# Rounding angles inside PSUM and packing small matmuls: an adaLN block with a state-space convolution

## The chip, the cores and the metric

The kernel runs on one core of a Trainium2 chip. The metric is the device time of one execution in microseconds. The engines named below are PE (TensorE: matmuls into PSUM), DVE (VectorE), ACT (ScalarE), POOL (GpSimd) and SP (SyncE, which here only issues DMAs, in order). Each engine works through its own instructions in order, and waits for others by semaphores. PSUM has eight banks of 128 x 512 fp32; this kernel uses six as a rotating pool ("pb", by the function `bank`) and two for the angles ("pa").

## The reference

The input x is 2048 rows (positions) of 512 channels. Six vectors of 512 come from `mod = silu(c) @ w_mod`: shift, scale and gate for two halves. The first half normalizes each row, scales and shifts it, and convolves each channel along the positions with its own kernel K; the second is an MLP.

```python
h = _layernorm(x) * (1 + ca) + sa
x = x + ga * _A_ref(h, ...)        # convolution with K, plus h * Dskip
h = _layernorm(x) * (1 + cb) + sb
x = x + gb * _B_ref(h, ...)        # Dense 512->1792, Mish, Dense 1792->512

# inside _A_ref, for each channel d and position l (N = 128 states):
P = jnp.exp(logdA[:, :, None] * l[None, None, :])     # complex
K = jnp.einsum("dn,dnl,dn->dl", Cc, P, dB).real
y = irfft(rfft(pad(u)) * rfft(pad(K)))[:L]            # linear convolution by FFT of 4096
```

P needs a magnitude (an exponential) and a phase (sine and cosine of an angle counted in turns, so only its fractional part matters).

## The kernel before, in words

**Blocks and steps.** The 512 channels are four blocks b of 128. Each block has eight groups of 16 channels, so there are 32 groups, and the main loop walks steps k = -1 to 40. A step runs one stage of each of many pipelines, each at its own offset (the table `ORDER`): for example the angles of group k+2, the kernel generation of group k-1, the Fourier stage of piece k-7. Every instruction gets a priority, 10000 times the step plus a fraction (`PRI0` for steps below 7, `PRI` later, otherwise the place in `ORDER`). A planner then lays out each engine's order and the turns of the buffers from these priorities with a cost model of its own.

**Angles (s_ang, s_ri, s_neg, s_sin).** For each group, PE forms 2 x 512 angles per partition as x, in turns, by four fp32r matmuls of 256 columns with the table `ac` (L341) into the two "pa" banks, of which there is one set. Then the whole number of turns is taken off. Adding and subtracting MAGIC = 1.5 * 2^23 in fp32 rounds to an integer. For 14 of the 32 groups (`RID` = 1) DVE does both at once, out of PSUM (L352). For the other 18, ACT adds MAGIC (L346) and DVE subtracts it (L354). The rounded value goes back to PE, which subtracts it by two fp16 matmuls with minus the identity (L359, `negid`). ACT then reads the angles as an absolute value (L364) and as a sine, which frees the banks, and makes the cosine from the first.

**Kernel generation.** DVE makes the magnitudes (s_mag, L374 and L377) and multiplies them in (s_comb, L384 to L388); PE contracts over the states (s_kgen, L399; 32-column outputs in four column groups) and does the first part of the Fourier transform of K (s_ka, L416). ACT copies in between.

**Input.** `stats` takes means and variances of 16 tiles XR[j] of 128 positions (12 on DVE, group 3 on ACT), `norm_scales` the reciprocal roots, `norm` (L505) normalizes in place. `ua(j, hf)` multiplies a tile by a 128 x 128 constant `bdu` on PE (L512), ACT copies the bank (L513), and after each second tile SP writes to the DRAM scratch `ud` (L515). These stand in steps 1 to 4. From step 6 on, `s_gl` reads `ud` back in another order.

**Modulation.** For each vector four pieces of w_mod come in; for each, four f32 matmuls use the piece as weights and move a single column (L445), ACT copies 4 columns (L449), and `mod_sum` on DVE adds the pieces.

**Fourier stage and back.** For each piece v (32 in all) PE transforms input and kernel (s_ubu, s_ubk, L530), DVE multiplies (s_prod), PE transposes (s_t1), inverts (s_invb, L579), ACT copies, SP writes to scratch `zd` (L582; two halves for each block). For each block, after its eight pieces, s_zl reads it back as `zt` in four tiles (L590; the halves land in a tile's two rows of 512), s_inva does the last inverse by two f32 matmuls of 128 rows and 512 columns for each tile (L614), DVE adds the input (L616, loaded by s_xp through `x_rows`, L192) and SP writes x2d (L617).

**Tail and MLP.** After the loop the last block's zl and inva, the second layernorm (ln_stats, ln_norm, ln_t) and the MLP over four tiles of 512 positions (L868, L886).

An f32 matmul shows in the trace as two records, each with its own weight load; fp32r, bf16 and fp16 ones as one.

Of the kernel before, what the change touches and what calls it, by code (L numbers as in the profile page):

```python
# [10 lines left out]
F32 = mybir.dt.float32  # L11
# [7 lines left out]
P = 128  # L19
# [15 lines left out]
BN = [0, 0, 0, 1]  # L35
NS = 1
SPA = 0
RID = [1, 0, 0, 0, 1, 0, 0, 0, 1, 0, 0, 0, 1, 0, 0, 1, 1, 0, 0, 0, 1, 1, 0, 1, 1, 0, 1, 0, 1, 1, 0, 1]
PRI = {"mm": 0.933, "ug": 0.775, "tm": 0.608, "inva": 0.817, "sin": 1.075, "ml": 0.533, "st": 0.933, "par": 0.625, "ri": -0.108, "kgen": 0.05, "p": -0.475, "sr": 1.575, "t2": 0.15, "ls": 0.275, "ut": 0.675}
PRI0 = {"comb": 0.675, "mc": 0.133, "sm": -0.167, "ua": 0.008, "par": 0.675, "ut": 0.583, "mm": 0.383, "inva": 1.717, "ka": 1.258, "ang": 0.067, "neg": 0.533, "ri": -0.067, "mag": 0.467}  # L40
# [6 lines left out]
    ("kgen", 1), ("ks", 1), ("ubu", 7), ("ang", -2), ("gl", 6), ("ri", -2), ("misc", 0), ("zl", 13),  # L47
    ("mag", -1), ("t1", 9), ("ka", 1), ("par", 0), ("tm", 1), ("neg", -2),
# [4 lines left out]
def _constants():  # L53
# [14 lines left out]
    di = np.zeros((2, 2, 4, 16, 32, 4))  # L68
    for t in range(4):
        bdk[t, :, :, t, :] = da  # L70
        for hf in range(2):
            for c in range(2):
                di[hf, c, t, :, :, t] = da[:, c, 16 * hf:16 * hf + 16].T / 2048.0
    bdu = bdk.transpose(1, 0, 2, 3, 4)
# [13 lines left out]
    for e in range(3):  # L88
# [13 lines left out]
        "bdu": np.ascontiguousarray(bdu.reshape(P, 8, 2, 16).transpose(0, 2, 3, 1)).reshape(P, 256).astype(f),  # L102
        "di": np.ascontiguousarray(di.transpose(3, 1, 2, 0, 4, 5)).reshape(P, 256).astype(f),
# [14 lines left out]
def s4_block(ctx, tc, io, out):  # L118
# [71 lines left out]
    def x_rows(dst, j0, n, b=None):  # L190
        w = D if b is None else P
        nc.sync.dma_start(dst, view(io["A_u"], j0 * D + (0 if b is None else b * P),  # L192
                                    [[16 * D, P], [D, n], [1, w]]))

    bdk = cst.tile([P, 256], F32, name="bdk")
    bdu = cst.tile([P, 256], F32, name="bdu")
    di = cst.tile([P, 256], F32, name="di")
# [9 lines left out]
    negid = gen.tile([P, P], F16, name="negid", bufs=1)  # L207
    magic = const_col(MAGIC, "magic")
# [123 lines left out]
    EC, PA, RI, MG = {}, {}, {}, {}  # L332

    def s_ang(k):
        b, c = divmod(k, 8)
        p = psum.tile([P, 2, 512], F32, tag="pa", name="pang", bufs=1)
        PA[k] = p
        for e in range(2):
            for q in range(2):
                g, o = 2 * q + c // 4, 8 * (c % 4)  # L340
                T.matmul(p[:, e, 256 * q:256 * q + 256], S12[b, g][:, e, :],  # L341
                         ac[:, 32 * o:32 * o + 256], start=(q == 0), stop=False, skip_group_check=True)
        EC[k] = gen.tile([P, 2, 16, 96], F32, tag="ec", name=f"ec{k}", bufs=3)
        if RID[k]:
            return
        A.activation(EC[k][:, :, :, 32:64], p.rearrange("p e (d x) -> p e d x", d=16), AF.Identity, bias=magic)  # L346

    def s_ri(k):
        ri = gen.tile([P, 2, 512], F16, tag="ri", name=f"ri{k}", bufs=1)
        RI[k] = ri  # L350
        if RID[k]:
            V.tensor_scalar(ri, PA[k], MAGIC, MAGIC, op0=OP.add, op1=OP.subtract)  # L352
            return
        V.tensor_scalar(ri.rearrange("p e (d x) -> p e d x", d=16), EC[k][:, :, :, 32:64], MAGIC, None,  # L354
                        op0=OP.subtract)

    def s_neg(k):
        for e in range(2):
            T.matmul(PA[k][:, e, :], negid, RI[k][:, e, :], start=False, stop=True, skip_group_check=True)  # L359

    def s_sin(k):
# [3 lines left out]
        act(ang[1], pv, AF.Sin, scale=TWO_PI)  # L365
# [67 lines left out]
    WM = {}  # L433
    mcol = gen.tile([P, 24, KB], F32, name="mcol", bufs=1)
# [7 lines left out]
    def mod_mm(n):  # L442
        p = bank("pmodp")
# [4 lines left out]
    def mod_cp(n):  # L448
        A.copy(mcol[:, n, :], WM[n][:, :NB])  # L449

    def mod_sum(s):
        t = mcol[:, 4 * s:4 * s + 4, :]
        V.tensor_add(t[:, 0:2], t[:, 0:2], t[:, 2:4])
        V.tensor_add(modp[:, s, :], t[:, 0], t[:, 1])
        if s in (2, 3):
            V.tensor_scalar(modp[:, s, :], modp[:, s, :], 1.0, None, op0=OP.add)
# [43 lines left out]
    SEG = 16 * P  # L500
    ud = dram.tile([2 * NB * P, SEG], F32, name="ud")
    zd = [[dram.tile([P, 16, P], F32, name=f"zd{b}{hf}") for hf in range(2)] for b in range(NB)]
# [4 lines left out]
    def ua(j, hf):  # L507
        if j % 2 == 0:
            US[j // 2, hf] = cv.tile([P, NB, 2, P], F32, tag="us", name=f"us{j}{hf}", bufs=2)
        t = US[j // 2, hf]  # L510
        p = bank("pua")
        T.matmul(p, bdu[:, P * hf:P * hf + P], XR[j], start=True, stop=True)  # L512
        A.copy(t[:, :, j % 2, :], p.rearrange("p (b d) -> p b d", b=NB))  # L513
        if j % 2:
            nc.sync.dma_start(view(ud, hf * NB * P * SEG + (j - 1) * P, [[SEG, P], [P * SEG, NB], [1, 2 * P]]),  # L515
                              t.rearrange("p b j d -> p b (j d)"))
# [456 lines left out]
```

## Time and profile before

| what | us |
|---|---|
| three runs | 749.09, 754.63, 756.65 (median 754.63) |
| the profiled execution | 749.49 |
| its span (first to last instruction) | 747.7 |
| busy in the span: PE, DVE, ACT | 659.3, 455.7, 358.4 |
| mean granted clock of PE | 0.966 |

A row of a group of instructions reads: line, engine, operation, out<-in, shapes, count | busy time in us, mean ns of one | idle time of that engine just before them, and what ended it. A row of the timeline reads: start, duration (both us), engine, line, and in brackets the idle time before and who ended it. A row of waits reads: who <- for whom, total us, how often, longest.

### The profile page before, as it was taken

Reading aid. Unit: us, or ns where it says so; the run is one execution under the profiler, and the core shown is the slowest. Engines: PE = TensorE matmul, PEld = TensorE weight load, DVE = VectorE, ACT = ScalarE, POOL = GpSimd, SP = SyncE. Lnnn points to the kernel's source line nnn. Section 1 sums busy time; section 2 is a strip of 40 time slices with the busy share of each in tenths; the row PEclk is TensorE's granted clock in tenths of the full one; section 3 lists DMA queues with packets and bytes.
Section 4 is the critical chain, followed back from the end, with each engine's and each line's share of the span. In section 5 each row is a group of like instructions: output and inputs, shape, how many; then the busy total and the mean of one; then the engine's idle time right before and its main releaser. Section 6 shows DMA issues by size and latency. Waiting matters only on the chain.

```text
span 747.7 us, 13563 instructions
## 1 busy us (share of the span) xinstructions
PE 659.3 (88%) x5472; PEld 517.5 (69%) x5472; DVE 455.7 (61%) x940; ACT 358.4 (48%) x565; POOL 51.7 (7%) x108
## 2 busy tenths in 40 slices
PE   0781998899987998999996699999999999999997
PEld 0560456688765777777764378888888888888885
DVE  5879726888999999999663785138111521152113
ACT  4753566887886688765552262232223322232221
POOL 1005002024203220000000000000000000000000
PEclk9985899899999999999999899999999999999999
DMA  9752575245424762355685760003100320002001
GB/s 307 248 196 46 159 263 156 72 121 141 123 58 115 195 173 73 104 167 170 200 265 169 232 205 1 0 2 121 47 1 0 106 64 1 0 12 74 0 1 57
DMA packets 87751, 83.09 MB, mean 111 GB/s; under 512 B 8836, under 2 KB 69256, under 8 KB 87048
## 3 DMA queue, kind: packets, MB, share of 16 engines
q1 hardware_dynamic: 80968, 78.35, 33.2%
q0 software_dynamic: 6720, 3.87, 2.9%
q8 instruction: 43, 0.70, 0.4%
q14 instruction: 20, 0.16, 0.1%
HBM read 54.93 MB, written 25.17 MB: 107 GB/s over the span
## 4 chain that ended last, share of the span: by engine, by line
PE 69%; DVE 16%; DMA 7%; ACT 6%; issue 1%; POOL 0%; SPq 0%; DVEq 0%; ACTq 0%; POOLq 0%
PE pm L868 20%; PE po L886 19%; PE pka L416 3%; PE pua L512 3%; PE pkg L399 3%; PE pub L530 3%; PE pkb L530 3%; PE pmodp L445 2%; PE pib L579 2%; PE pia L614 2%; DVE ec L388 2%; PE pang L341 2%; DVE q L564 2%; DVE ec L384 2%; PE pang L359 1%
## 5 line engine op out<-in xcount | busy, mean ns | idle before, releaser
L875 DVE TENSOR_TENSOR mal<-mh,mah 128x512 fp32r<-128x512 f32 x56 | 38.6, 691 | 177.1 <-ACT mah L874 176.7
L868 PE MATMUL pm<-hh,w1h 128*128 128x512 f32 x448 | 139.3, 392 | 2.8 <-ACT hh L779 2.8
L142 ACT ACTIVATE mh<-pm,b 128x512 f32<-128x512 f32 x56 | 38.5, 690 | 202.7 <-PE pm L868 202.7
L868 PEld LDWEIGHTS pm<-hh,w1h 128*128 128x128 f32 x448 | 84.6, 189 | 21.3 <-ACT hh L779 3.3
L868 PE MATMUL pm<-hh,w1l 128*128 128x512 f32 x224 | 87.9, 392 | 0.0
L886 PE MATMUL po<-w2h,mah 128*128 128x512 f32 x224 | 87.9, 392 | 0.0
L886 PE MATMUL po<-w2l,mah 128*128 128x512 f32 x224 | 87.6, 391 | 0.0
L886 PE MATMUL po<-w2h,mal 128*128 128x512 f32 x224 | 87.3, 390 | 0.0
L384 DVE TENSOR_TENSOR ec<-ec,m 128x1024 f32<-128x1024 f32 x32 | 39.0, 1219 | 20.0 <-ACT ec L142 19.8
L868 PEld LDWEIGHTS pm<-hh,w1l 128*128 128x128 f32 x224 | 42.5, 190 | 8.9
L886 PEld LDWEIGHTS po<-w2h,mah 128*128 128x128 f32 x224 | 42.0, 188 | 8.8 <-issue 0.4
L886 PEld LDWEIGHTS po<-w2h,mal 128*128 128x128 f32 x224 | 42.0, 188 | 8.5
L886 PEld LDWEIGHTS po<-w2l,mah 128*128 128x128 f32 x224 | 42.1, 188 | 8.3
L564 DVE TENSOR_TENSOR q<-pkb,ug 128x512 f32<-128x512 f32 x64 | 41.8, 683 | 6.3 <-PE pkb L530 6.2
L399 PE MATMUL pkg<-ec 128*32 128x64 f32 x2048 | 40.2, 228 | 4.5 <-DVE ec L388 4.5
L512 PE MATMUL pua<-xr,bdu 128*128 128x512 f32 x64 | 31.6, 642 | 13.6 <-DVE xr L505 13.1
L416 PE MATMUL pka<-bdk,ks 128*64 128x128 f32 x512 | 39.8, 286 | 3.4 <-DVE ks L405 3.4
L399 PEld LDWEIGHTS pkg<-ec 128*32 128x32 f32 x2048 | 34.4, 112 | 11.6 <-issue 7.3
L364 ACT ACTIVATE ec<-pang 128x1024 f32<-128x1024 f32 x32 | 32.9, 1027 | 15.0 <-PE pang L359 14.8
L530 PE MATMUL pkb<-mf,gk 128*128 128x128 f32 x256 | 37.8, 284 | 1.8 <-ACT gk L423 1.8
L374 DVE TENSOR_TENSOR m<-co 128x1024 f32<-128x1024 f32 x32 | 39.0, 1219 | 0.1
L388 DVE TENSOR_TENSOR ec<-ec,m 128x1024 f32<-128x1024 f32 x32 | 38.9, 1217 | 0.0
(164 smaller groups left out, 1154.6 us busy)
## 6 DMA issues: line engine op xcount, KB each, us to landing
ud<-us SPq DMA_DIRECT2D x16, 512.0 KB, 3.5
gu<-ud SPq DMA_DIRECT2D x32, 256.0 KB, 2.9
zd<-z SPq DMA_DIRECT2D x32, 256.0 KB, 2.6
zt<-zd SPq DMA_DIRECT2D x32, 256.0 KB, 4.1
wm<-in_w_mod SPq DMA_DIRECT2D x24, 256.0 KB, 2.9
out<-ot SPq DMA_DIRECT2D x16, 256.0 KB, 2.0
xp<-in_A_u SPq DMA_DIRECT2D x15, 256.0 KB, 3.3
x2d<-xp SPq DMA_DIRECT2D x15, 256.0 KB, 3.5
```

The costliest lines, as they stand in the source:

```text
L142: chain(A.activation(out, in_, f, **kw))
L374: V.tensor_mul(m2.rearrange("p d (a b) -> p d a b", a=8), co[:, :, 12:20, None].to_broadcast([P, 16, 8, 8]), co[:, :, None, 20:28].to_broa ...
L384: V.tensor_mul(ec[:, :, :, 32:64], ec[:, :, :, 95:63:-1], m2[:, None, :, 0:32].to_broadcast([P, 2, 16, 32]))
L388: V.tensor_mul(ec[:, :, :, 0:32], ec[:, :, :, 0:32], m1[:, None].to_broadcast([P, 2, 16, 32]))
L399: T.matmul(o, ec[:, z, e, 0:32], ec[:, z, e, 32:96], start=(z == 0), stop=(z == 1))
L416: T.matmul(pv[64 * cc:64 * cc + 64, :, o:o + 4], KS[k][:, 64 * m:64 * m + 64], bdk[:, 128 * cc:128 * cc + 128], start=True, stop=True)
L512: T.matmul(p, bdu[:, P * hf:P * hf + P], XR[j], start=True, stop=True)
L530: T.matmul(pv[:, :, r, :], lh(r), mf[:, 4 * s + r, :].rearrange("p (c s) -> p c s", c=2), start=not started, stop=True, skip_group_check=s ...
L564: V.tensor_mul(q, kv[:, c, :, None, :].to_broadcast([P, 4, 2, 64]), ug)
L868: T.matmul(p, w1[wi][:, k, fs], hh[:, hi, k, :], start=(n == 0), stop=(n == 3 * KB - 1))
L875: V.tensor_sub(a[1], h, a[0])
L886: T.matmul(PO[tt][q], a[ai][:, P * q:P * q + P], w2[wi][:, f, :], start=(f == 0 and n == 0), stop=(f == FB - 1 and n == 2))
```

## The change

1. **Angles.** s_ri and s_neg go, and with them the ACT pass of s_ang. Everything becomes one accumulation in PSUM: x by `ac` (four matmuls), plus MAGIC and minus MAGIC as two bf16 matmuls of 512 columns for each half (ones times MAGIC/128 over 128 rows), minus x by `nac` = -`ac` (four matmuls). What stays is round(x) - x, and the sine's scale turns its sign.
2. **Input.** Positions are laid out anew over the partitions (32 rows of 64 positions each, four groups a). `ua(g)` multiplies 32 rows by 64 columns: eight f32 matmuls in four row groups and two column halves, into four banks at once; four ACT copies into tiles borrowed from several tags; eight DMAs of 512 B runs to `ud`.
3. **Last inverse.** zd is one scratch per block; a `zt` tile holds two column halves of 64 rows; s_inva works on pairs of the former tiles: eight matmuls of 64 rows and 32 columns into two banks. x_rows of one block becomes four DMAs.
4. **Modulation.** The vector silu(c) is the weight (32 equal columns), the w_mod piece moves, 512 columns, the four pieces in four column groups of one bank; one ACT copy; the sum over the groups by four matmuls against a column of 1/32 and one DVE operation.
5. **Order.** stats(3) moves to step 0, norm_scales and norm get priorities ahead (-0.6, -0.4) in step 1, ua gets 0.7 in place of 0.008 and goes by g, two per step; the load order of the tiles changes.

```diff
-BN = [0, 0, 0, 1]
+BN = [0, 0, 0, 0]
-PRI0 = {"comb": 0.675, "mc": 0.133, "sm": -0.167, "ua": 0.008, ...
+PRI0 = {"no": -0.6, "nr": -0.4, "comb": 0.675, "mc": 0.133, "sm": -0.167, "ua": 0.7, ...
...
+        for a in range(4):
+            nc.sync.dma_start(dst[32 * a:32 * a + 32], view(io["A_u"], (16 * a + j0) * D + b * P,
+                                                            [[64 * D, 32], [D, n], [1, P]]))
...
+        o = 8 * (c % 4)
         for e in range(2):
-            for q in range(2):
-                g, o = 2 * q + c // 4, 8 * (c % 4)
-                T.matmul(p[:, e, 256 * q:256 * q + 256], S12[b, g][:, e, :],
-                         ac[:, 32 * o:32 * o + 256], start=(q == 0), stop=False, skip_group_check=True)
+            for w in (ac, nac):
+                for q in range(2):
+                    T.matmul(p[:, e, 256 * q:256 * q + 256], S12[b, 2 * q + c // 4][:, e, :],
+                             w[:, 32 * o:32 * o + 256], start=(w is ac and q == 0), stop=(w is nac),
+                             skip_group_check=True)
+                for z in range(2) if w is ac else ():
+                    T.matmul(p[:, e, :], oneb.to_broadcast([P, P]), rnd[:, z:z + 1].to_broadcast([P, 512]),
+                             start=False, stop=False, skip_group_check=True)
...
-        act(ang[1], pv, AF.Sin, scale=TWO_PI)
+        act(ang[1], pv, AF.Sin, scale=-TWO_PI)
...
     def mod_mm(n):
-        p = bank("pmodp")
-        for b in range(NB):
-            T.matmul(p[:, b:b + 1], WM[n][:, b * P:b * P + P], sc[:, n % KB:n % KB + 1], start=True, stop=True)
-        WM[n] = p
+        s, k = divmod(n, KB)
+        if k == 0:
+            PM[s] = bank("pmodr")
+        T.matmul(PM[s][32 * k:32 * k + 32, :], sc[:, k:k + 1].to_broadcast([P, 32]), WM[n], start=True, stop=True)
...
-    def ua(j, hf):
...
+    def ua(g):
+        ps = [bank("pua") for a in range(4)]
+        for h in range(2):
+            for a in range(4):
+                r = slice(32 * a, 32 * a + 32)
+                T.matmul(ps[a][64 * h:64 * h + 64, :], bdu[r, :], XR[8 * h + g][r, :], start=True, stop=True)
+        for a in range(4):
+            tag = ("us", "ug", "us", "xp", "ug", "us", "xp", "q1")[(4 * g + a) % 8]
+            t = cv.tile([P, NB, P], F32, tag=tag, name=f"us{g}{a}", bufs={"us": 3, "q1": 1}.get(tag, 2))
+            A.copy(t.rearrange("p b d -> p (b d)"), ps[a])
+            for h in range(2):
+                nc.sync.dma_start(view(ud, (16 * a + 8 * h + g) * P, [[64 * P, 64], [64 * 64 * P, NB], [1, P]]),
+                                  t[64 * h:64 * h + 64])
...
-        p = bank("pia")
-        for hf in range(2):
-            T.matmul(p, di[:, P * hf:P * hf + P], ZT[b, j4][:, hf, :], start=(hf == 0), stop=(hf == 1))
+        ps = [bank("pia") for h in range(2)]
+        for a in range(4):
+            for h in range(2):
+                r = slice(64 * h, 64 * h + 64)
+                T.matmul(ps[h][32 * a:32 * a + 32, :], di[r, :], ZT[b, j4 - 1, a // 2 * 2][r, a % 2, :], start=True, stop=True)
...
-    for n, j in enumerate((12, 13, 14, 15, 8, 9, 10, 11, 0, 1, 2, 3, 4, 5, 6, 7)):
-        at(NS, norm, j)
-        for hf in range(2):
-            at(NS + n // 4, ua, j, hf)
+    for n, g in enumerate((4, 5, 6, 7, 0, 1, 2, 3)):
+        for h in range(2):
+            at(NS, norm, 8 * h + g)
+        at(NS + UO + n // 2, ua, g)
```

More of the change, by code (lines that the diff above doesn't have):

```diff
@@ L206, in s4_block @@
     halfpi = const_col(HALF_PI, "halfpi")
-    negid = gen.tile([P, P], F16, name="negid", bufs=1)
-    magic = const_col(MAGIC, "magic")
+    oneb = cst.tile([P, 1], BF16, name="oneb")
+    nc.gpsimd.memset(oneb, 1.0)
+    rnd = cst.tile([P, 2], BF16, name="rnd")
+    for z in range(2):
+        nc.gpsimd.memset(rnd[:, z:z + 1], (1 - 2 * z) * MAGIC / P)
+    nac = gen.tile([P, 1024], F32R, name="nac", bufs=1)
     dt = cst.tile([P, NB], F32, name="dt")
@@ L635, in s4_block @@
     params(0, 3)
-    V.tensor_scalar(negid, ident, -1.0, None, op0=OP.mult)
+    V.tensor_scalar(nac, ac, -1.0, None, op0=OP.mult)
     load_s(0, 0)
```

119 lines of the change are left out of this document (46 added, 73 removed).

## The prediction

> **What bounds the kernel now.** I read the page first, its 40 slices, then a table of busy times by stage (columns: stretch, length, then busy time and instruction count of PE, PEld, DVE, ACT and, where it works, POOL; granted clock, DMA share, GB/s).
>
> ```profile
> span 747.7 us, 13563 instructions
> PE   0781998899987998999996699999999999999997
> ```
>
> ```profile
> core 0: us, PE busy (x) PEld busy (x) DVE busy (x) ACT busy (x) POOL busy (x), PEclk, DMA share, GB/s
> 0.00:39.00 39.00, 15.63 (x52) 11.37 (x52) 28.77 (x111) 21.45 (x41) 2.80 (x12) 1.00 0.79 267
> 39.00:121.00 82.00, 62.41 (x549) 37.94 (x548) 55.08 (x132) 42.65 (x77) 12.21 (x24) 0.83 0.53 172
> 121.00:180.00 59.00, 53.06 (x757) 43.67 (x757) 48.45 (x92) 47.08 (x78) 16.36 (x32) 0.94 0.44 119
> 180.00:340.00 160.00, 146.13 (x2122) 116.59 (x2123) 156.72 (x249) 121.23 (x177) 20.35 (x40) 0.99 0.45 125
> 340.00:426.00 86.00, 67.53 (x598) 49.99 (x596) 57.21 (x119) 34.44 (x53) 0.00 (x0) 0.96 0.66 203
> 426.00:747.70 321.70, 314.52 (x1400) 257.91 (x1400) 109.48 (x241) 91.56 (x141) 0.00 (x0) 0.99 0.13 44
> ```
>
> The last row is the MLP, PE at 98%; the change leaves its instructions alone (only the rows of the output move). So everything happens in the first 426 us, and there no one engine rules. In 39 to 121 us (where the input is transformed) no engine is over 76% busy. In 180 to 340 us DVE is 98% busy and idle for 3.3 us in all, with PE close behind at 91%. In 340 to 426 us neither is full.
>
> Slice 3 of the PE line is a 1. The waits of PE in that place, and the timeline, name the cause:
>
> ```profile
> PE pua L512 <- DVE xr L505: 13.1, 2, 12.7
> ```
>
> ```profile
> 73.84 1.22 PE L512 MATMUL pua<-xr,bdu 128*128 128x512 f32 x1 [12.70 <-DVE xr L505]
> ```
>
> The input matmuls stand in PE's order ahead of everything else of their step, and wait 12.7 us for normalized rows that DVE reaches late.
>
> **The change part by part.** First what can be priced from rows; the lines by form give count, busy time and mean ns.
>
> ```profile
> L512 PE MATMUL pua<-xr,bdu 128*128 128x512 f32 x64 | 31.6, 642 | 13.6 <-DVE xr L505 13.1 <-ACT us L513 0.5
> L346 ACT ACTIVATE ec<-pang,magic 128x1024 f32<-128x1024 f32 x18 | 20.1, 1116 | 6.6 <-PE pang L341 6.6
> L513 ACT COPY us<-pua 128x512 f32<-128x512 f32 x32 | 17.4, 597 | 30.5 <-PE pua L512 18.9 <-DMA ud<-us 11.6
> L352 DVE TENSOR_SCALAR ri<-pang 128x1024 f16<-128x1024 f32 x14 | 17.1, 1220 | 1.6 <-PE pang L341 1.3
> L354 DVE TENSOR_SCALAR ri<-ec 128x1024 f16<-128x1024 f32 x18 | 12.5, 692 | 10.3 <-ACT ec L346 10.1
> ```
>
> And one step of PE in the steady part, with two rows of a later place (start, duration). I use start to next start as an operation's real price, since the shown durations overlap.
>
> ```profile
> 299.67 1.17 PE L399 MATMUL pkg<-ec 128*32 128x64 f32 x64
> 300.77 0.38 PE L537 MATMUL pub<-su,sab 32*128 32x512 bf16 x1
> 301.08 1.16 PE L530 MATMUL pub<-mf,gu 128*128 128x128 f32 x8
> 302.00 0.72 PE L341 MATMUL pang<-ac,s 128*128 128x256 f32 x4
> ...
> 304.91 0.59 PE L359 MATMUL pang<-ri,negid 128*128 128x512 f16 x2
> 305.34 0.61 PE L530 MATMUL pkb<-mf,gk 128*128 128x128 f32 x4
> ```
>
> ```profile
> 371.28 1.88 PE L614 MATMUL pia<-zt,di 128*128 128x512 f32 x4
> 373.00 1.05 PE L579 MATMUL pib<-yt,mi 128*128 128x128 f32 x8
> ```
>
> *Angles.* Gone: 29.6 us of DVE (L352 and L354) and 20.1 us of ACT (L346) over 32 steps, and on PE the two matmuls with negid, 305.34 - 304.91 = 0.43 us a step. Added on PE: four 512-column bf16 matmuls at half of that 0.43, 0.86 us, and four more 256-column ones at 0.11 us (half the columns, half the price), 0.45 us. Net +0.88 us of PE per step, 28 us in all. So a load moves from DVE to PE.
>
> *Packing.* An f32 matmul of 512 columns is two records, 0.43 us each ((373.00 - 371.28)/4). Do packed ones run side by side? Kernel generation (L399) already uses four column groups: 64 records of 64 columns take 1.10 us. Eight records of 128 columns take 0.92 us (301.08 to 302.00), so 64 of 64 columns one after another would take 3.7 us: it runs 3.3 wide. For groups of rows no row shows it. Bounds for one input group of 8 matmuls: 0.86 us if all are parallel, 3.44 us if only the two column halves are, 6.9 us if none is; today's same work is 3.44. For the inverse (two row groups, four column groups): 0.86, 1.72 and 6.9 us a pair, today 3.44. I take full overlap plus 0.3 us for entering and leaving the packed form, since that is nearest to the L399 row: 1.15 us each. That entry cost has a row: L399 overlaps its successor by 0.07 us (299.67 + 1.17 against 300.77), L530 by 0.24, so a change of form costs about 0.17. The Trainium skill, TensorEngine Tiling (Array Packing), Key Properties, says that changing the tiling mode drains TensorE, and the rows agree; without that rule the sum would be some 5 us lower on PE, which changes little.
>
> *Modulation.* Today and in the two stages that hold most of it:
>
> ```profile
> 39.00:121.00 82.00, 11.39 (x80) 11.19 (x80) 1.22 (x10) 0.83 0.53 172
> 121.00:180.00 59.00, 11.53 (x96) 11.50 (x96) 1.67 (x12) 0.94 0.44 119
> ```
>
> Eight records of one load become one 512-column matmul, four of them in column groups, plus 8 short records a vector (0.12 us each, 11.53/96) for the sum. Two loads arrive together, so I count 0.86 us a pair: 3.4 us saved in the second stage, about 3 in the first. If nothing packs, 0.86 a load costs about what it does today. ACT and DVE copies shrink by under 1 us each: nothing.
>
> *Stage 39 to 121.* DVE falls by the ri work of this stretch (first row below, PE then DVE): 51 us. PE: -31.6 + 8 x 1.15 for the input, -3 modulation, +4.4 for five angles: 41 us. ACT about 37 us; the 32 copies (L513) stay.
>
> ```profile
> 39.00:121.00 82.00, 4.03 (x11) 4.00 (x5) 0.83 0.53 172
> 180.00:340.00 160.00, 11.64 (x38) 18.00 (x19) 0.99 0.45 125
> ```
>
> ```profile
> ud<-us SPq DMA_DIRECT2D x16, 512.0 KB, 3.5
> ```
>
> ```profile
> 99.88 0.39 SPq L515 DMA_DIRECT2D ud<-us  x1
> ```
>
> ```profile
> L505 DVE TENSOR_SCALAR xr<-xr,mv,rstd 128x512 f32<-128x512 f32 x16 | 7.5, 543 | 0.0
> ```
>
> DMA: 0.53 x 82 = 43 us of full use. The 8.4 MB of ud go out in runs of 512 B instead of 1 KB. Stages give the two rates: 172/0.53 = 325 GB/s here, 125/0.45 = 278 in the steady part (512 B runs mostly): +4 us, 48 in all. So the floor is 51 us, a gain of 31. The busiest engine now reaches 76% of the stage; at that share 51 us become 67, a gain of 15. The 12.7 us wait alone lies under both. I take 20. Of the norms brought ahead, 16 DVE instructions of 0.54 us now stand before a step's combination, so kernel generation is late by up to 7.5 us once; the 27 us in which DVE has nothing to do in this stage cover it. Norms issue no DMA; the input step now issues 64 on SP instead of 16 (0.39 us each, 19 us more over four steps), past the w_mod and parameter loads, for which the queue has room. If it had not, modulation sums would be late, due two steps after.
>
> *Stages 121 to 180 and 180 to 340.* In the long stage there are 1152 L399 records, 18 steps:
>
> ```profile
> 180.00:340.00 160.00, 21.37 (x1152) 18.42 (x1152) 0.99 0.45 125
> ```
>
> ```profile
> 180.00:340.00 160.00, 13.17 (x28) 4.78 (x28) 4.77 (x7) 0.99 0.45 125
> ```
>
> DVE falls by its 18.0 us of ri from 156.7 to 138.7. PE: 146.1 + 18 x 0.88 - 13.2 (28 records of the last inverse) + 3.5 x 1.15 = 152.8. **PE takes DVE's place**, and the floor is 152.8; with the 3.3 us that today's leader idles, 156: a gain of 4, not 18. In 121 to 180: 53.1 + 7 x 0.88 - 3.4 = 55.9 of 59: no gain. ACT's 20 us hide behind both and give nothing.
>
> *Stage 340 to 426.* Three to four steps carry last inverses at 1.72 us, on a PE that waits through short chains; two packed pairs save 4 x 1.72 - 2 x 1.15 = 4.5. At the end it turns round:
>
> ```profile
> 405.94 3.32 PE L614 MATMUL pia<-zt,di 128*128 128x512 f32 x6
> ...
> 407.11 0.38 SPq L582 DMA_DIRECT2D zd<-z  x1
> ...
> 412.60 4.21 PE L614 MATMUL pia<-zt,di 128*128 128x512 f32 x6 [3.34 <-DMA zt<-zd]
> ```
>
> Today half the last block is loaded and multiplied before the last z is written (zd has two halves). With one zd, two whole tiles load after it: I charge 2 us. Net gain 2.5.
>
> *At nothing:* xp loads in four DMAs (SP is mostly idle; without that cover 1.1 us a piece), the smaller constants, nac (one DVE operation while the parameters load), the store pattern (same 2 KB runs).
>
> Sum: 20 + 0 + 4 + 2.5 = 26.5 us off the profiled execution's 749.5 (span 747.7): 723. That execution is near the lowest of the runs, whose median is 5.1 higher; I add half of that and forecast **726**.
>
> **The rivals.** *DVE keeps setting the pace in the steady part*, because PE's gaps there are slack: 138.7 + 3.3 = 142, 14 us more: 712. For it: DVE had 98%. Against: PE's 91%.
>
> *The ud writes bind.* The first read of ud needs all of them; 30 us of writes (8.4 MB at 278 GB/s) from about 55 us, with the w_mod loads between them, end near 110: the stage gains 8: 738. For it speaks the wait of ACT on ud (11.6 us in the L513 row).
>
> *The order does not move.* A priority only proposes; if PE still meets the input before the norms, the 12.7 us remain: 739.
>
> *A strict order in PE.* If a matmul never starts before its predecessor, the second record of one tile holds back the next tile: 8 x 0.43 = 3.44 us a group, as now. The stage then gains 12, the steady part loses 4, the tail 2: 746. The L399 rows speak against it: four records stand in a row for each column group, and strict order would give 16 x 3 x 0.057 = 2.7 us where 1.10 is measured. The Trainium skill, TensorE: Matmul & The Clock Gate, Part 3, says that matmuls start and end strictly in program order; this trace disagrees.
>
> *Slower: PSUM banks.* An input group takes four of six banks at once, and the modulation row holds a fifth until a step later. PE then waits in order for ACT's copies: behind a step's three activations (3.2 us) four copies take 2.4, 5.6 us a group. It decides where eight such waits fill what PE has free, 82 - 41 = 41 us, that is from 5.1 us a group. At 7.5 us (kernel generation waiting for its bank too) PE has 101 us in that stage: 19 us longer instead of 20 shorter: 765. For it: ACT already waits and is waited for here. Against: the groups are spread over four steps.
>
> **How the numbers follow.** Chances: forecast 0.42, DVE pace 0.17, ud 0.15, order 0.08, strict order 0.06, banks 0.12. About 1% (747 to 762) is what a measurement can tell from no change. Faster by more takes the first four and some of the strict order: 0.83; within 1%: 0.06; slower: 0.11. Range: 708 (the DVE pace, and 4 of the 11 us that the first stage has left to its floor) to 748 (up to strict order), leaving out the slower case and some extremes.
>
> **What would show it.** Right: no PE wait on xr of over 3 us; eight input records in about 1 us; in the steady part PE busier than DVE, DVE idle some 20 us in 18 steps, the step 8.5 to 8.8 us. Wrong: 3.4 us or more per packed group (packing fails); PE waiting on copies of us (banks); DVE still at 98% (its pace stayed); the first gu load waiting on ud.

## The result, and the profile after

The changed kernel takes **785.25 us** (median of 4 runs, 784.37 to 786.42) against 755.09 for the kernel before on the same chip: ratio 1.0416, 95% interval 1.0357 to 1.0474. It is slower by 4%, where the forecast was 726 us. The profiled execution is the one of 784.37 us. From its page, the span and PE's 40 slices:

```profile
span 782.6 us, 14045 instructions
PE   0427897799999999999855799997999899989991
```

The stages are cut at the same events as before: the second, seventh, fourteenth and last angle step (the absolute values on ACT) and the first MLP matmul. Columns as in the prediction's table: stretch, length, busy time and count of PE, PEld, DVE, ACT and POOL, granted clock, DMA share, GB/s.

```profile
0.00:49.00 49.00, 13.98 (x48) 9.15 (x48) 19.29 (x94) 22.41 (x46) 2.91 (x15) 0.91 0.40 128
49.00:116.00 67.00, 47.86 (x482) 25.11 (x485) 55.51 (x118) 29.53 (x45) 12.06 (x24) 0.73 0.65 195
116.00:192.00 76.00, 66.12 (x873) 45.14 (x863) 54.04 (x108) 48.51 (x76) 16.23 (x32) 0.96 0.63 159
192.00:344.00 152.00, 149.25 (x2245) 123.35 (x2244) 142.00 (x233) 111.62 (x167) 20.48 (x40) 1.00 0.48 126
344.00:437.00 93.00, 68.52 (x667) 48.87 (x665) 51.43 (x110) 35.10 (x54) 0.00 (x0) 0.87 0.66 193
437.00:782.60 345.60, 317.89 (x1400) 259.13 (x1400) 110.13 (x243) 91.84 (x142) 0.00 (x0) 0.97 0.14 41
```

| stage | before | after | difference | forecast |
|---|---|---|---|---|
| start | 39 | 49 | +10 | 0 |
| input transform | 82 | 67 | -15 | -20 |
| next 7 steps | 59 | 76 | +17 | 0 |
| 18 steady steps | 160 | 152 | -8 | -4 |
| tail | 86 | 93 | +7 | -2.5 |
| MLP | 321.7 | 345.6 | +24 | 0 |

The differences make up the 35 us of the spans. The two stages from which the forecast took its gain did gain. The largest loss is in the MLP, whose instructions did not change, and the second largest is right behind the first gain.

**The MLP.** Its one new thing is the pattern of the output store. From the views of waits, after and then before (who <- for whom, total us, times, longest):

```profile
DVE ot L903 <- DMA out<-ot: 29.1, 8, 5.5
```

```profile
DVE ot L904 <- DMA out<-ot: 2.5, 3, 0.9
```

DVE waits for the tile `ot`, since the store before has not landed. One such stretch of after, as a window, and what PE does before and at its end in the timeline:

```profile
526.70:533.50 6.80, 2.96 (x14) 2.11 (x12) 2.58 (x6) 1.31 (x2) 0.00 (x0) 0.90 0.33 82
```

```profile
519.75 0.39 PE L867 MATMUL pm<-hh,w1l 128*128 128x512 f32 x1
...
534.36 1.22 PE L867 MATMUL pm<-hh,w1h 128*128 128x512 f32 x2 [4.70 <-DVE ot L903]
535.38 0.63 PE L867 MATMUL pm<-hh,w1l 128*128 128x512 f32 x1
```

At a DMA share of 0.33 82 GB/s are moved, PE stands for 4.70 us, and then a matmul record takes 0.63 us where one before it took 0.39: the stall is paid a second time in clock (granted 0.58 from 534 to 540 us, 1.00 from 515 to 525). Most of the 24 us are the stalls themselves: PE's busy time in the MLP grows by only 3.4 us, from 314.5 to 317.9.

**The start.** The five loads of x have the same outermost count of 4. The DMA queue of SP, after and before, then a window of each while x comes in:

```profile
4.47 26.62 SPq L189 DMA_DIRECT2D xr<-in_A_u  x5
...
39.20 15.99 SPq L694 DMA_DIRECT2D mf<-in_mf  x1
```

```profile
4.56 6.97 SPq L192 DMA_DIRECT2D xr<-in_A_u  x5
```

```profile
21.00:31.00 10.00, 1.56 (x7) 1.38 (x8) 3.59 (x19) 5.31 (x13) 0.00 (x0) 1.00 0.25 107
```

```profile
11.00:20.00 9.00, 0.00 (x0) 0.00 (x0) 7.30 (x34) 7.87 (x15) 0.00 (x0) 1.00 1.02 423
```

A share of 0.25 fits four of 16 engines, at 107 GB/s, and all later loads queue behind it on SP: `mf` starts at 39.20 us in place of 23.35, and the first loads of w_mod at 55.23 in place of 16.33, so that PE waits for them:

```profile
63.49 3.81 PE L440 MATMUL pmodr<-wm,sc 128*32 128x512 f32 x8 [14.51 <-DMA wm<-in_w_mod]
```

The Trainium skill (DMA: Bandwidth & Descriptors, Why a DMA increments its semaphore by 16 and not by 1) states that a transfer runs on the largest number of engines, up to 16, that divides the outermost counts of both its patterns. By that rule 4 outside gives four engines, and the share of 0.25 agrees. The prediction didn't weigh it.

### The profile page after: what moved, and what is told of

The parts are those of the page before. It is cut to its first block, busy times and chain, and to the rows that moved or that the text cites. A ratio compares the mean times of both kernels' runs of the same rounds, so it can differ in the third digit from the quotient of the medians.

```text
span 782.6 us, 14045 instructions
## 1 busy us (share of the span) xinstructions
PE 663.6 (85%) x5696; PEld 510.8 (65%) x5696; DVE 432.4 (55%) x900; ACT 339.0 (43%) x529; POOL 51.7 (7%) x111
## 4 chain that ended last, share of the span: by engine, by line
PE 69%; DMA 10%; SPq 8%; DVE 6%; ACT 4%; issue 1%; POOL 0%; DVEq 0%; ACTq 0%; POOLq 0%
PE pm L867 18%; PE po L885 17%; PE pkg L392 4%; PE pub L525 4%; PE pang L346 4%; DMA out<-ot 4%; PE pkb L525 3%; PE pka L409 3%; SPq L189 3%; PE pib L574 3%; PE pang L350 3%; SPq L694 2%; PE pmodr L440 2%; PE pt L566 2%; DMA wm<-in_w_mod 1%
## 5 line engine op out<-in xcount | busy, mean ns | idle before, releaser
L867 PE MATMUL pm<-hh,w1h 128*128 128x512 f32 x448 | 141.1, 396 | 7.0 <-DVE ot L903 4.7
L350 PE MATMUL pang<-rnd,oneb 128*128 128x512 bf16 x128 | 41.7, 410 | 0.0
L346 PE MATMUL pang<-nac,s 128*128 128x256 f32 x128 | 39.4, 390 | 0.0
L409 PE MATMUL pka<-bdk,ks 128*64 128x128 f32 x512 | 38.0, 280 | 1.3 <-DVE ks L398 1.3
L525 PE MATMUL pub<-mf,gu 128*128 128x128 f32 x256 | 37.1, 288 | 1.6 <-DMA gu<-ud 1.6
```

The source lines that it names most:

```text
L346: T.matmul(p[:, e, 256 * q:256 * q + 256], S12[b, 2 * q + c // 4][:, e, :], w[:, 32 * o:32 * o + 256], start=(w is ac and q == 0), stop=(w ...
L350: T.matmul(p[:, e, :], oneb.to_broadcast([P, P]), rnd[:, z:z + 1].to_broadcast([P, 512]), start=False, stop=False, skip_group_check=True)
L409: T.matmul(pv[64 * cc:64 * cc + 64, :, o:o + 4], KS[k][:, 64 * m:64 * m + 64], bdk[:, 128 * cc:128 * cc + 128], start=True, stop=True)
L525: T.matmul(pv[:, :, r, :], lh(r), mf[:, 4 * s + r, :].rearrange("p (c s) -> p c s", c=2), start=not started, stop=True, skip_group_check=s ...
L867: T.matmul(p, w1[wi][:, k, fs], hh[:, hi, k, :], start=(n == 0), stop=(n == 3 * KB - 1))
```

## Experiments

### The two patterns

The first kernel splits the store into four plain DMAs of 32 partitions, the second the x loads in the same way, the third does both:

```diff
-        nc.sync.dma_start(view(out, (4*tt + q)*D, [[16*D, 4], [64*D, 32], [1, D]]), o...)
+        for a in range(4):
+            nc.sync.dma_start(view(out, (16*a + 4*tt + q)*D, [[64*D, 32], [1, D]]), o[32*a:32*a + 32]...)
```

> The changed kernel with one edit: each store of the output is four DMAs of 32 partitions, each with a plain pattern, instead of one whose pattern counts 4 on the outside and 32 inside. Theory (a DMA whose outer count is 4 is served by a few DMA engines only, near 100 GB/s at a share of 0.25): the MLP, 345 us from its first matmul to the end in the changed kernel, comes back to 321 to 324, and the time falls by 20 to 25 us, to 760 to 765. Rival (the MLP is slow because the clock or the buffers changed): it stays at 340 or more and the time within 5 us of 785.

> The changed kernel with one edit: the five loads of the input rows are four DMAs of 32 partitions each. Theory: the loads are issued within 10 us instead of 27, the first angles' activation comes back from 37 us to about 29, w_mod is no longer late and PE no longer waits 20 us for it; the time falls by 15 to 30 us, to 755 to 770. Rival (the lateness before step 9 comes from the 64 writes to ud on the SP queue, or from the packed forms): only the 9 us at the start come back, 776.

> Both edits. Theory: the sum of both gains, 735 to 748, near or under the kernel before (755). If the packed matmuls or the angles are what costs, it stays above 760.

The next two turn it round: only the store's pattern is changed in the kernel before, to 4 x 32 rows and to 16 x 8 rows. The rows of the output come out permuted; the work is the same.

```diff
-view(out, (4*tt + q)*D, [[16*D, P], [1, D]])
+view(out, (4*tt + q)*D, [[16*D, 4], [64*D, 32], [1, D]])     # first kernel
+view(out, (4*tt + q)*D, [[16*D, 16], [256*D, 8], [1, D]])    # second kernel
```

> The kernel before with one edit: the output store's pattern on the DRAM side counts 4 on the outside, 32 inside, as in the changed kernel. The same rows of 2 KB are written, but rows come out at other positions, so that the output is a permutation of the reference's. Theory: the MLP alone becomes 20 to 25 us longer, the time 775 to 780. Rival (it is not the pattern): within 3 us of 755.

> The kernel before, with the pattern of the output store counting 16 outside (16 x 8 rows) in place of 128 rows; the rows of the output come out permuted. If the number outside sets how many of the 16 DMA engines share a transfer (four where it is 4: share 0.25, about 100 GB/s), then 16 uses all of them: 754 to 757 us, and an L904 store takes about 2 us. If any second level in the pattern slows it, it comes near the 777 us of the pattern that counts 4 outside.

| kernel | median us | ratio to before |
|---|---|---|
| changed | 785.25 | 1.0416 (1.0357 to 1.0474) |
| its store split | 762.4 | 1.0084 (1.0051 to 1.0117) |
| its x loads split | 782.28 | 1.0345 (1.0307 to 1.0383) |
| both split ("mended") | 757.31 | 1.0027 (1.0004 to 1.005) |
| before, store with 4 outside | 777.14 | 1.0267 (1.0226 to 1.0307) |
| before, store with 16 outside | 756.86 | 1.0 (0.9957 to 1.0044) |

From the waits of the last two in the MLP, first 4 outside, then 16:

```profile
DVE ot L904 <- DMA out<-ot: 28.2, 8, 5.5
```

```profile
DVE ot L904 <- DMA out<-ot: 6.5, 5, 1.8
```

The store's pattern costs 23 us in the changed kernel and 22 in the one before, and nothing with 16 outside. So it is the outermost count, not the second level or the order of rows. The load pattern costs 3 to 5 us. **That explains the 4%, but the mended kernel only equals the one before.** The 26 us of gain are still missing.

The theories of the store (760 to 765 us) and of both rows of the store's pattern in the kernel before (775 to 780, 754 to 757) held. Those of the x loads fell: they were to be worth 15 to 30 us, and both together were to give 735 to 748. With the x loads split PE's longest wait for w_mod falls from 14.5 to 5.6 us, but in the same place there now stands one of 16.0 us for `ks`, a small tile that DVE makes. The split of the store isn't free either, it seems: from the start of the last matmul to the end of the span 8.4 us pass in the mended kernel and 5.8 in the one before, and the last stores take SP 8.18 us (16 issues) in place of 5.29 (4).

### Where the gain of the mended kernel went

In the trace of the mended kernel PE has a hole (timelines of PE and of DVE):

```profile
73.69 0.69 PE L409 MATMUL pka<-bdk,ks 128*64 128x128 f32 x2 [16.59 <-DVE ks L398]
```

```profile
66.07 7.50 DVE L498 TENSOR_SCALAR xr<-xr,mv,rstd 128x512 f32<-128x512 f32 x16
73.49 0.15 DVE L398 TENSOR_TENSOR ks<-ks,dtap 128x4 f32<-128x4 f32 x1
```

The norms stand as one block in front of the small addition that PE waits for, and ahead of them, from 54.8 us on, the 12 statistics of DVE and the inverse root: 18.7 us in all. Four kernels each change one thing in the mended one: statistics, norms and input step placed as before (BN, `no`, `nr`, `ua`); the old rounding put back; `ud` laid out for runs of 2 KB; half of the writes issued from ACT.

```diff
-BN = [0, 0, 0, 0]          PRI0: "no": -0.6, "nr": -0.4, "ua": 0.7       # old order
+BN = [0, 0, 0, 1]          PRI0: "ua": 0.008
-view(ud, (16*a + 8*h + g)*P, [[64*P, 64], [64*64*P, NB], [1, P]])        # 2 KB runs
+view(ud, (16*a + 8*h + g)*NB*P, [[64*NB*P, 64], [1, NB*P]])
-nc.sync.dma_start(view(ud, ...                                           # two queues
+(nc.scalar if h else nc.sync).dma_start(view(ud, ...
```

> The changed kernel with both patterns mended (757.3 us), and with the places of statistics, norms and input step as before. In the mended kernel PE idles 16.6 us at 73 us behind a block of 12 statistics, the inverse root and 16 norms on DVE, and the 64 ud writes end at 131 us. Theory: the ud writes set the end of the stage in either order, since DMA is at 0.78 to 0.85 meanwhile: 754 to 761 us, with the hole moved but not gone. Rival: the new order was worth something: 763 us or more. Second rival: the block costs what it idles PE: 740 to 745 us.

> The mended kernel (757.3 us) with the angles rounded as before (on DVE and ACT, negid matmuls on PE), all else as in the change. Theory: in the 18 steps from 181 to 340 us of before, the new angles gave the 7.2 us seen, and DVE's rounding returns to the first stage with little cost, since the ud writes bind there: 763 to 769 us; DVE 98% busy in the steady part again. Rival: the steady gain came from packing: 755 to 759 us.

> The mended kernel (757.3 us), with ud laid out so that the four channel blocks of a position lie side by side: an ud write has runs of 2 KB in place of 512 B, a read of it 512 B runs as now, 2 KB apart. Theory (the ud writes bind the stage that ends with the first read): the 64 writes take some 30 us in place of 47.7, the first input step of the convolution comes over 10 us earlier: 743 to 748 us. Rival (PE's or DVE's own work binds there): 755 to 758 us.

> The mended kernel (757.3 us) with the ud writes of the upper 64 partitions issued from ACT's queue in place of SP's. The 64 writes take 47 us, 0.73 us each, with 512 B runs or 2 KB runs alike. Theory: SP's issue of so many writes sets that rate and holds back the loads of w_mod behind them: the writes end some 10 us earlier, 748 to 753 us. Rival (the DMA engines at 0.8 or PE's own work set it): 755 to 759 us, or up to 765 us through ACT's 0.4 us of issue for each of 32 writes.

Old order: 764.61 (1.0117, 1.0057 to 1.0177); the new order is worth 7 us here, the first rival. Old rounding: 766.3 (1.0145, 1.0076 to 1.0214), 9 us, as the theory had it. Runs of 2 KB: 755.15 (1.0014, 0.9979 to 1.005): the bytes of ud don't bind, the theory fell. Two queues: 773.35 (1.0237, 1.019 to 1.0283), 16 us slower, above both theory (748 to 753) and rival (up to 765). There each write costs ACT what it costs SP (rows of a line: count, min/median/max ns, first and last start):

```profile
L511 ACTq DMA_DIRECT2D ud<-us x32: 582/607/1744, 84.2 to 141.7; - x32
```

```profile
L511 SPq DMA_DIRECT2D ud<-us x64: 574/620/1476, 84.0 to 131.1; - x64
```

The first row is of this kernel, the second of the mended one. That is 19 us more on ACT (32 x 0.607), and the last write is issued at 141.7 in place of 131.1. The Trainium skill (DMA: Bandwidth & Descriptors, Issuing engines are not separate DMA queues) says that several issuing engines save only issue time. No faster writes show here either. Whether SP's time for the issues sets the pace of the writes stays open, since this run delays ACT's copies as well.

Three attempts at the hole and the tail: 8 of DVE's 12 statistics forced ahead of the first combination and 8 norms on ACT; z in two halves, each loaded on its own; both together with the 2 KB runs.

```diff
+        if k == 0: the first combination stands behind the statistics of groups 1 and 2
+        if j % 2: A.activation(XR[j], XR[j], AF.Identity, scale=rstd..., bias=nmr...)   # norm
-    zd = [dram.tile([64, 64*P]) for b ...]
+    zd = [[dram.tile([32, 64*P]) for e in range(2)] for b ...]
```

> The changed kernel with both patterns mended (757.3 us); 8 of the 12 statistics that DVE makes are put ahead of the first combination, into the 6.45 us that DVE idles there (28.8 to 35.2 us), and 8 of the 16 norms go to ACT. Theory: the 16.6 us that PE waits at 73 us are DVE's block of statistics, inverse root and norms; it gets some 9 us shorter, and with it the ud writes and all that follows come earlier: 748 to 752 us, PE's wait on ks 6 to 9 us. Rival (the hole is made up later, since the loads of w_mod and ud set the pace after it): 755 to 759 us though the wait shrinks.

> The mended kernel (757.3 us) with z in two halves again, each loaded by DMAs of its own (32 partitions), the packed matmuls as they are. In the mended kernel PE waits 7.15 us for zt at the end of the convolution and then makes the last 32 packed matmuls in 9.2 us at half clock, where before made them in between. Theory: half of the last loads go ahead of the last z, the wait falls to 3 to 4 us and the clock stays higher: 751 to 754 us. Rival (the second half sets the end alone): 756 to 759 us.

> The three of them that touch no queue together: ud in 2 KB runs, early statistics with half the norms on ACT, z in two halves. If the stalls add up as single prices (2 + 7 + 4 us off 757.3): 744 us, faster than before by 1.5%. If one bottleneck takes over from the other: 750 to 755 us.

They took 766.39 (1.016, 1.0106 to 1.0214), 766.84 (1.0153, 1.0092 to 1.0214) and 770.06 (1.0201, 1.0163 to 1.0238): all slower, against both theory and rival. In the first the idle 6.45 us were not filled: a small instruction of DVE that waits 7.55 us for ACT (L694) came to stand ahead of the statistics. They ran where the combinations had run, and PE's hole became longer (19.36 us). So this run does not test the theory. In the second kernel the loads of z behind the last z take SP little longer than in the mended one (13 loads in 8.87 us, 8 in 8.16). But the last z itself is issued at 422.48 us in place of 410.00, though the last angle step starts at the same time (339.2 and 339.5). So the loss arises between the two. PE waits there for zt, 4.85 us in one piece at 393 us, which it doesn't in the mended kernel; whether that is the cause stays open.

### The parts one by one, in the kernel before

Angles need 2 KB more per partition; the control gets it by writing `ud` once per position and half (32 writes in runs of 2 KB). On it come the new angles, then the packed modulation, then the new order; input step and last inverse stay unpacked. From there, one kernel adds the packed input step with its loads, their order and its writes (and one `xp` tile fewer than the change), another the packed last inverse with its layouts (and `bdu` in a tile that `sel` leaves).

```diff
 # control
-view(ud, hf*NB*P*SEG + (j - 1)*P, [[SEG, P], [P*SEG, NB], [1, 2*P]])
+view(ud, hf*P*NB*SEG + j*D, [[NB*SEG, P], [1, D]])
 # then, one on the other: s_ang / s_sin of the change; mod_mm, mod_cp, mod_sum of the change; BN and PRI0 of the change
 # then either: ua, x loads (20 DMAs), ud of the change;  or: zd, s_zl, s_xp, s_inva of the change, store in 4 DMAs
```

> The kernel before (755 us) with its input step writing ud once per position and half (32 writes of 256 KB in runs of 2 KB in place of 16 of 512 KB in runs of 1 KB), which frees the 2 KB per partition that the new angles need. A control: 752 to 758 us, if neither size nor number of writes binds in the stage of before. If the number of issues binds (16 more at 0.4 us), up to 762 us.

> The control with the new angles alone: no packing, old order, old patterns. Theory: the angles are worth the 9 us that they are worth in the mended kernel: 8 to 10 us below the control, 744 to 748 us, most of it in the 18 steps from 180 to 340 us (7 us). Rival (in before PE's packed places are needed for them, since PE gets 28 us of added work): 753 us or more.

> The new angles and the packed modulation rows in the control. Theory (by the price of the prediction, 3.4 us of PE in the stage of 121 to 180 and 3 us before): 2 to 5 us below the run with the angles alone. Rival: no difference within 2 us, since the mean over 32 rows adds 8 short matmuls and a copy, and the loads of w_mod set the pace.

> Angles, modulation and the new order together in the control, with input step and last inverse unpacked. Theory: the order is worth the 7 us that it is worth in the mended kernel: 733 to 740 us, 2% faster than before, so that the packed pair with its transfers costs the mended kernel about 20 us. Rival (the order pays only for packed input groups): no difference to the run before, or slower by up to 5 us.

> The kernel of 735.1 us (angles, modulation, order) with the packed input step: x in 20 loads, 8 packed groups, 64 writes of ud at 0.6 us of SP each; last inverse and output as before. Theory: the writes keep SP for some 40 us, the last one ends near 131 us in place of some 121, and the w_mod loads behind them hold PE: 745 to 752 us. Rival (the step itself is cheap, the tail costs all): 733 to 738 us.

> The kernel of 735.1 us with the packed last inverse: z in one piece, z loads with 0.60 us of issue in place of 0.42, 60 input loads in place of 15, and an output store in four DMAs; input step as before. Theory: the tail waits about 7 us for the last z and makes 32 packed matmuls at half clock: 741 to 747 us. Rival (packed inverses save PE their 1.7 us a piece in the steady part): 728 to 735 us.

| kernel | median us | ratio to before |
|---|---|---|
| control | 753.92 | 0.9987 (0.9955 to 1.002) |
| + angles | 746.79 | 0.9911 (0.9869 to 0.9953) |
| + modulation | 743.83 | 0.9867 (0.9811 to 0.9923) |
| + order | 735.05 | 0.9737 (0.9688 to 0.9786) |
| + packed input step | 756.93 | 1.0034 (1.0002 to 1.0065) |
| + packed last inverse instead | **733.04** | **0.9711** (0.9653 to 0.9768) |

The control and the three kernels on it come out as their theories had it, with one exception: the angles' gain is not in the steady steps (below) but ahead of them, the fourth angle step starting at 47.08 us in place of 56.65. The packed input step costs more than its theory (745 to 752 us), and for the packed last inverse the rival (728 to 735) holds. **The packed input step costs 22 us and takes with it all that the other parts gain; without it the change is faster by 3%.** The last row is the fastest kernel of the study. The 3 us of the modulation and the 2 us of the inverse lie within the intervals.

Where the 22 us arise shows in three kernels: with the old order ("+ modulation"), with the new one, and with the packed input step. First norms on DVE, then the reads of ud (count, min/median/max ns, first to last start); for the last two kernels the statistics too.

```profile
L500 DVE TENSOR_SCALAR xr<-xr,mv,rstd x16: 528/536/606, 62.8 to 69.8; 128x512 f32<-128x512 f32 x16
L512 SPq DMA_DIRECT2D gu<-ud x32: 359/377/560, 112.2 to 377.3; - x32
```

```profile
L664 DVE BATCH_NORM_STATS2 bst<-xr x12: 657/675/687, 20.5 to 32.7; 128x6 f32<-128x512 f32 x12
L500 DVE TENSOR_SCALAR xr<-xr,mv,rstd x16: 539/541/543, 43.3 to 50.2; 128x512 f32<-128x512 f32 x16
L507 SPq DMA_DIRECT2D ud<-us x32: 319/320/392, 56.9 to 101.9; - x32
L512 SPq DMA_DIRECT2D gu<-ud x32: 359/377/587, 103.1 to 368.0; - x32
```

```profile
L674 DVE BATCH_NORM_STATS2 bst<-xr x12: 676/677/696, 55.3 to 63.1; 128x6 f32<-128x512 f32 x12
L503 DVE TENSOR_SCALAR xr<-xr,mv,rstd x16: 529/536/582, 66.6 to 73.5; 128x512 f32<-128x512 f32 x16
L516 SPq DMA_DIRECT2D ud<-us x64: 574/622/1913, 84.0 to 134.4; - x64
L522 SPq DMA_DIRECT2D gu<-ud x32: 359/377/2133, 137.3 to 393.7; - x32
```

The new order brings the norms from 62.8 to 43.3 us and the first read of ud from 112.2 to 103.1. With the packed input step the statistics, which had stood between the first parameters at 20.5 us, come at 55.3, behind four combinations. So the norms start 23 us later, the writes 27 us later; 64 writes take 50 us in place of 45, and the first read comes 34 us later. But PE never waits for what is read from ud (`gu`), and the kernel is 22 us later, not 34. What PE does wait for are these two:

```profile
74.19 0.69 PE L413 MATMUL pka<-bdk,ks 128*64 128x128 f32 x2 [15.92 <-DVE ks L402]
135.50 1.88 PE L444 MATMUL pmodr<-wm,sc 128*32 128x512 f32 x2 [6.14 <-DMA wm<-in_w_mod]
```

They are the hole behind DVE's block and the w_mod loads behind the writes on SP. In the "+ order" kernel PE waits at most 0.4 us at a time for `ks` in this stretch, and not for w_mod. The angle steps agree: the seventh starts 19 us later than in the "+ order" kernel (109.81 and 90.37), the fourteenth and the last some 25 later, and the spans differ by 25 as well (755.5 and 730.5). The two waits together are 22 us, as long as the loss; that is no proof, since a wait need not all be lost, and PE waits for ACT's angles 5 us longer too. And the 20 loads, the order of the tiles, the 64 writes and the packed matmuls came in one edit; no run separates them. Why the statistics moved is only partly shown. In the mended kernel the 20 loads start on SP between 4.5 and 23.9 us and land 7.9 us later, so by some 32 us. Late arrival alone thus doesn't make it 55; the order in which DVE's instructions stand does. That the planner set this order because it prices the 20 loads as late wasn't tried.

## Why the prediction was wrong, by its own steps

**"At nothing: ... the store pattern (same 2 KB runs)"** is the step that failed most: 23 us. The runs were indeed the same; the number of engines follows the outermost count. No cover was named for it: `ot` has two buffers, so DVE waits up to 5.5 us for the tile of an earlier store, and PE behind DVE.

**The x loads were not in the sum at all.** Their pattern costs 3 to 5 us. With split loads and the packed input step, the statistics stand behind four combinations; that the split alone does it isn't shown.

**"... kernel generation is late by up to 7.5 us once; the 27 us in which DVE has nothing to do in this stage cover it"** failed too, and the wait that it left out is the longer of the two behind the 22 us. The price counted the 16 norms alone. In the mended kernel 12 statistics and the inverse root stand in the same block, 18.7 us, and DVE's idle time elsewhere in the stage doesn't cover it: PE waits 16.6 us in one piece (15.9 in the kernel with the packed input step alone). In the changed kernel PE waits for `ks` only 1.3 us there, and 19.8 for w_mod, which comes late.

**"I take 20" for the input transform.** The changed kernel gains 15 there, but starts 10 later. The floor behind it, 31 us, was right: with the order working, the stage of the "+ order" kernel, from its second angle step to its seventh, is

```profile
38.00:90.00 52.00, 47.24 (x422) 26.32 (x424) 46.96 (x105) 31.74 (x47) 12.01 (x24) 0.93 0.64 208
```

52 us in place of 82, DVE at 47.0 where the sum had 51. That kernel's input step is unpacked: the gain came from the order and the angles, not from packing, to which the prediction gave 31.6 - 8 x 1.15 us of PE. Part of it is given back right after, where the forecast had 0: 71 us in place of 59. PE is busy for 67 of them, with the new angles and with 16 input records (L505, 7.1 us) that now fall into this stage:

```profile
90.00:161.00 71.00, 67.15 (x859) 46.46 (x855) 50.89 (x93) 48.24 (x74) 16.25 (x32) 1.00 0.43 122
```

**64 issues at "0.39 us each, 19 us more", "for which the queue has room".** They were counted for SP and charged to nobody. The size was off, and so was the cover. After, and before:

```profile
L511 SPq DMA_DIRECT2D ud<-us x64: 574/622/1375, 87.8 to 137.0; - x64
```

```profile
L515 SPq DMA_DIRECT2D ud<-us x16: 359/360/387, 80.5 to 119.7; - x16
```

64 x 0.62 = 40 us of SP in place of 16 x 0.36 = 6, with the w_mod loads behind them, for which PE waits (the second such wait of this kernel):

```profile
141.00 1.91 PE L440 MATMUL pmodr<-wm,sc 128*32 128x512 f32 x2 [5.33 <-DMA wm<-in_w_mod]
```

The rate of bytes, on which the rival of the ud writes rested, isn't it: runs of 2 KB changed nothing.

**"The order does not move"**, given 0.08, describes the changed kernel in part. The 12.7 us that PE waited for xr shrink to 3.7 in all (longest 2.6), as forecast, but the norms start at 81.0 us against 73.2 before (rows of the lines, after and before), and PE waits for w_mod instead. In the unpacked kernel the order moves the norms by 20 us, and PE's wait for xr goes from 13.7 us to none: there the forecast had the mechanism right.

```profile
L498 DVE TENSOR_SCALAR xr<-xr,mv,rstd x16: 540/542/543, 81.0 to 87.8; 128x512 f32<-128x512 f32 x16
```

```profile
L505 DVE TENSOR_SCALAR xr<-xr,mv,rstd x16: 528/536/606, 73.2 to 80.2; 128x512 f32<-128x512 f32 x16
```

**The steady steps: right in mechanism, better than priced.** "PE takes DVE's place" is what the windows of 18 steps show: the control, angles alone, old angles with all packing, and the mended kernel.

```profile
184.50:345.00 160.50, 145.14 (x2116) 115.60 (x2115) 155.64 (x248) 120.97 (x175) 20.38 (x40) 0.99 0.45 124
```

```profile
177.00:337.00 160.00, 155.99 (x2204) 127.42 (x2221) 144.57 (x240) 112.05 (x167) 20.43 (x40) 1.00 0.45 124
```

```profile
186.00:342.00 156.00, 137.71 (x2110) 110.63 (x2109) 151.98 (x243) 118.54 (x174) 20.41 (x40) 0.97 0.47 122
```

```profile
187.70:339.50 151.80, 149.05 (x2244) 123.17 (x2243) 141.76 (x232) 111.53 (x167) 20.55 (x40) 1.00 0.49 126
```

Angles alone change who leads (DVE 155.6 to PE 156.0) and gain nothing in this stage; packing alone gains 4; only together they gain 8 to 9. PE came to 149, not 152.8, and the step to 8.4 us, not 8.5 to 8.8; DVE to 142, not 138.7. The terms: the new angles add 0.60 us of PE a step (145.1 to 156.0 in 18 steps) where the sum had 0.88, and the packed inverse takes off 7.0 us (156.26 to 149.25, below) where it had 13.2 - 3.5 x 1.15 = 9.2. The rival of DVE's pace (14 us more) is out.

**The tail.** "I charge 2 us" for the single zd was too little. The last tiles wait 7 us for z, whose eight loads follow one another on SP for 8.1 us (from 386.39 on), and they run at a granted clock of 0.58 (390 to 398 us); what each of the two costs isn't separated (fastest kernel):

```profile
390.12 7.11 PE L607 MATMUL pia<-zt,di 64*32 64x512 f32 x24 [7.16 <-DMA zt<-zd]
```

Steady steps and tail of the "+ order" kernel, and of the fastest one:

```profile
161.00:322.00 161.00, 156.26 (x2205) 127.66 (x2223) 143.68 (x238) 112.05 (x167) 20.48 (x40) 1.00 0.43 122
322.00:410.00 88.00, 70.52 (x625) 52.25 (x624) 50.75 (x105) 35.90 (x56) 0.00 (x0) 0.96 0.68 205
```

```profile
161.00:313.00 152.00, 149.25 (x2246) 123.27 (x2243) 141.98 (x232) 111.54 (x167) 20.57 (x40) 1.00 0.49 127
313.00:406.00 93.00, 70.70 (x669) 50.72 (x667) 51.45 (x109) 34.74 (x54) 0.00 (x0) 0.86 0.68 194
```

The tail takes back 5 of the 9 us that the packed inverse gains in the steady steps, and the MLP, with the split store, most of the rest (324.3 us to the end of the span in place of 320.5).

**The packed group** was priced at 1.15 us. In place it takes about 1.5 at full clock: 24 records, one and a half groups, in 2.20 us from start to start. Within these the 16 records of the whole group start over 0.91 us (120.62 to 121.53); the half group behind them takes the rest. A pair of the packed last inverse takes 1.01 us (230.47 to 231.48, fastest kernel). So the price was near, and somewhat high where a group is issued whole.

```profile
120.62 2.27 PE L505 MATMUL pua<-xr,bdu 32*64 32x512 f32 x24
122.82 0.50 PE L346 MATMUL pang<-ac,s 128*128 128x256 f32 x2
```

So packing works in both directions of the array. The strict order (3.44 us) is out, and no wait of PE on copies of us of the size that the slower rival needed (5.1 us a group) shows, the longest being 1.9 us (packed input step alone): the kernel was slower for another reason.

## What to carry to other kernels

Price every transfer whose layout an edit touches, even if its bytes and runs stay: its outermost count, its number of issues on the queue, and what its arrival moves in the order of the engines. A gain on an engine that waits in one stage is worth what the next hand-over lets through; here these are the tile `ks`, which stood behind DVE's block of statistics and norms, and the w_mod loads, which stood behind the writes on SP. And test the parts of a combined change singly: all of these but one made a kernel 21 us faster, and the one took it back.

## What the runs showed that was not expected

- Four loads of 32 partitions are slower than one of 128 at the same share. In the mended kernel, while the 20 loads run, the window shows share 1.00 at 205 GB/s, against 1.02 at 423 above for the kernel before:

```profile
15.00:31.00 16.00, 9.62 (x36) 6.37 (x36) 11.86 (x45) 9.46 (x25) 0.00 (x0) 0.97 1.00 205
```

- An issue on SP took 0.32 us for the plain write of 128 partitions, 0.36 for before's with three levels, and 0.60 to 0.62 (medians) for the writes of 64 partitions, with runs of 512 B and 2 KB alike.
